# A two-pass channel gate: last load of pass one split in two, first scaling pieces cut finer, pass two reordered

## The chip, the core and the metric

The kernel runs on one core of one Trainium2 chip. The metric is the device time in microseconds. TensorE is called PE in the profile, VectorE DVE, ScalarE ACT, GpSimd POOL and SyncE SP. A "row" below is one image row of the work's tiling: 384 bf16 values on each of 128 partitions, 98,304 bytes in all.

## The reference

```
B, H, W, C = x.shape            # 1, 384, 384, 384, bf16
g = jnp.einsum("bhwc->bc", x) / (H * W)
s = _sigmoid(g * w1d[0])        # k = 1: no neighbours, no padding
return x * s[:, None, None, :]
```

Every channel is averaged over all pixels, the average is scaled by one weight and put through a sigmoid, and the whole input is multiplied by that gate. No element of the output can be written before the last element of the input has been read.

## The kernel before, in words

The 147,456 pixels make 1152 rows. SBUF holds `ROWS` = 275 rows in one tile, `arena`; the input does not fit, so there are two passes.

**Pass one** loads all 1152 rows. PE adds each with a matmul of ones into one PSUM bank (`sum_rows`, L291). 780 "stream" rows are dropped after that, and 372 are kept: 59 raw, the others in groups that DVE folds from four rows into three rows' room (`fold`, L331), with ACT testing that the folding is without loss. The last loads of pass one are written out by hand in L495: pairs of a row number in `arena` and a length. `U`, `V`, `W`, `A`, `T`, `Y` name places in `arena` (108, 212, 232, 220, 259, 267); `take_raw` loads and sums. After row 1152 ACT makes the gate `s_bf` (L503) and copies it to PSUM (`s_ps`, L507).

**Pass two** stores 1152 rows and loads the 780 stream rows again, all from the one queue of SP: `load` (L267), `store` (L525). `scale` (L512) multiplies in place. DVE scales nearly everything and unfolds the groups (`unfold`, L535); POOL scales 13 raw rows, A+26 to A+38, beside DVE at the start. While POOL works, DVE reads the gate from PSUM, later from SBUF.

The order of pass two is made by a loop that runs when the program is built (L771 to L849). It keeps a clock of its own, takes costs per row for DVE and DMA, and appends scales, unfolds, loads and stores to each engine's list. `landed` (L692) says in which pieces DVE scales the raw rows, `alongside` (L700) what POOL scales and when its store is due; a piece with `end` True gets a store of its own. A load may be appended when rows of `arena` have been stored. Each engine then runs its list strictly in order, waiting on semaphores: SP waits for DVE or POOL ahead of a store, and for a store's landing ahead of a load that overwrites its rows. DMA number n of SP, counted from 0, signals the semaphore `f_SP` followed by n modulo 24.

Of the kernel before, what the change touches and what calls it, by code (L numbers as in the profile page):

```python
# [145 lines left out]
def kernel(  # L146
# [13 lines left out]
    B, H, W, C = x.shape  # L160
# [14 lines left out]
    U = 3 * PIECE + PAIRS * 3 * PAIR  # L175
    G0 = U + PAIR
    V = G0 + PAIRS * 3 * PAIR
    A = V + PAIR
    N_A = 39
    T = A + N_A  # L180
    Y = T + 2 * PIECE
# [14 lines left out]
    W = A + 3 * PIECE  # L196
# [63 lines left out]
    def raw(a):  # L260

        return c_raw + (a - U if a < G0 else PAIR + a - V if a < A else 2 * PAIR + a - W)
# [202 lines left out]
    LATE = [(W + 4, 8), (U, 8), (W + 12, 8), (W + 20, 7)]  # L465
# [25 lines left out]
    def take_raw(a, n):  # L491
        load(raw(a), a, n)
        return sum_rows(a, n)

    for a, n in [(V, 8), *LATE, (W, 4), (T, 4), (T + 4, 4), (Y, 4), (Y + 4, 2), (Y + 6, 2)]:  # L495
        step = take_raw(a, n)
        if a == Y - 4:
            fl.hold("DVE", 2 * N_DVE[1], step)
# [13 lines left out]
    def scale(a, n, eng="DVE", s=s_bf, after=()):  # L512
        v = arena[:, a : a + n, :]
        vec = nc.vector if eng == "DVE" else nc.gpsimd
        step = fl.add(
            eng,
            lambda: vec.tensor_tensor(  # L517
                out=v, in0=v, in1=s[:, None, :].to_broadcast([P, n, C]), op=Op.mult
            ),
            reads=rows(a, n) + ["s_bf" if s is s_bf else "bank0"], writes=rows(a, n), after=after,  # L520
        )
        if eng == "DVE":
            scales.append(step)
# [165 lines left out]
        return f  # L689


    for a, n, end in ((Y, 2, True), (Y + 2, 2, True), (Y + 4, 4, True), (U, 4, True), (U + 4, 4, True), (T, 8, True), (V, 8, True)):  # L692
        landed.append((a, raw(a), n, end))
    landed.append((W, raw(W), 8, True))
    landed.append((W + 8, raw(W + 8), 6, True))
# [1 line left out]

    alongside = deque()
    t = 1.0
    for a, n in ((A + 26, 4), (A + 30, 4), (A + 34, 5)):  # L700
        scale(a, n, "POOL", after=[copied])
        t += 0.2 + 0.84 * n
        alongside.append((t, a, raw(a), n))
# [67 lines left out]
    while True:  # L771

        if dve_at <= now:
# [4 lines left out]
            if landed and (ahead < PENDING or not can):  # L778
                a, at, n, end = landed.popleft()
# [13 lines left out]
        if alongside and alongside[0][0] <= now:  # L793
            _, a, at, n = alongside.popleft()
# [3 lines left out]
        while waiting and waiting[0][0] <= now:  # L798
            _, n, then, at, a, known = waiting.popleft()
# [10 lines left out]
        if bank_at is None and len(line) <= total - BANKS_AT and got and max(got)[0] >= N_BANKED:  # L810
            a = max(got)[1]
# [11 lines left out]
        if got and todo < N_STREAM:  # L823
            n, a = max(got)
            left = N_STREAM - todo
            left -= run_of(left - 1)[0]
            n = min(n, CAP, left)
# [57 lines left out]
```

## Time and profile before

| | |
|---|---|
| median of three runs | 719.55 us (719.46 to 719.58) |
| the profiled execution: its own time / its span | 718.83 us / 717.1 us |
| busy: DVE / PE / ACT / POOL | 475.2 / 213.0 / 121.4 / 10.2 us |
| SP's DMA queue | 303.18 MB, 99.1% of 16 engines' span |
| mean rate | 423 GB/s |

The profile cuts the span into windows; for each it gives the busy time of every engine, the granted clock of PE, the mean busy share of the 16 DMA engines and the GB/s moved. The chain of waits follows back from the last instruction what each step waited for. The timeline lists instructions by start and length. SP's entries (SPq) are the issuing of DMAs, not the transfers.

### The profile page before, as it was taken

The page shows a single profiled execution, that of the slowest core. Times are in us where ns is not written, and L with a number is a line of the kernel's source. Part 1 is how long each engine was busy: PE and PEld are TensorE (multiplying, and loading weights), DVE is VectorE, ACT ScalarE, POOL GpSimd, SP SyncE. Part 2 cuts the span into 40 slices and gives each one's busy share as a digit, 9 for nine tenths or more (in the row PEclk, how much of TensorE's full clock was granted, in tenths as well). Part 3 has the DMA queues.
Part 4 walks back from the last instruction along what each step waited for, and adds up shares of the span by engine and source line. Part 5 has one row for each costly group of instructions (what it writes and reads, how often), then busy time and mean ns, then how long its engine had stood idle before and what let it go on. Part 6 is the DMA issues. An engine that isn't in the chain of part 4 may idle for free.

```text
span 717.1 us, 2040 instructions
## 1 busy us (share of the span) xinstructions
PE 213.0 (30%) x1186; PEld 0.3 (0%) x3; DVE 475.2 (66%) x355; ACT 121.4 (17%) x97; POOL 10.2 (1%) x7
## 2 busy tenths in 40 slices
PE   4776978998869780000000000000000000000000
PEld 0000000000000000000000000000000000000000
DVE  4606280639896829999999999779966960128900
ACT  3704160426674610000110000000000000000000
POOL 0000000000000005000000000000000000000000
PEclk9998989999999996555555555555555555555555
DMA  9999999999999989999999999999999999999997
GB/s 373 436 426 440 424 442 426 439 429 420 428 430 425 427 358 355 406 424 431 433 428 422 444 424 445 423 439 428 439 420 435 433 433 436 436 432 431 437 421 343
DMA packets 21038, 303.31 MB, mean 423 GB/s; under 512 B 2338, under 2 KB 2850, under 8 KB 9378
## 3 DMA queue, kind: packets, MB, share of 16 engines
q1 hardware_dynamic: 21024, 303.18, 99.1%
q8 instruction: 4, 0.07, 0.0%
q14 instruction: 8, 0.07, 0.0%
q10 hardware_dynamic: 2, 0.00, 0.0%
HBM read 189.92 MB, written 113.25 MB: 423 GB/s over the span
## 4 chain that ended last, share of the span: by engine, by line
DMA 56%; DVE 23%; PE 7%; another core or an unknown queue 3%; ACT 2%; POOL 1%; SPq 1%; issue 0%; DVEq 0%
DMA arena<-in_x_dram 45%; DVE arena L517 17%; DMA out_dram<-arena 11%; PE bank L280 7%; DVE arena L315 4%; ACT arena L352 2%; DVE arena L321 2%; POOL arena L517 1%; SPq L274 1%; SPq L531 0%; ACT s_bf L503 0%; ACT bank L507 0%; ACT bank L429 0%; DVEq L124 0%
## 5 line engine op out<-in xcount | busy, mean ns | idle before, releaser
L517 DVE TENSOR_TENSOR arena<-arena,s_bf 128x6144 bf16<-128x6144 bf16 (+13 forms) x67 | 226.9, 3424 | 86.1 <-DMA arena<-in_x_dram 71.0
L280 PE MATMUL bank<-arena,ones 128*128 128x384 bf16 x1151 | 207.2, 342 | 46.2 <-DMA arena<-in_x_dram 45.6
L315 DVE TENSOR_SCALAR arena<-arena 128x1536 uint16<-128x1536 uint16 (+4 forms) x193 | 136.9, 763 | 107.6 <-DMA arena<-in_x_dram 94.9
L352 ACT ACTIVATE arena<-arena 128x3072 uint16<-128x3072 uint16 (+1 forms) x38 | 107.6, 2831 | 111.6 <-DVE arena L315 111.6
L321 DVE TENSOR_TENSOR arena<-arena 128x1536 uint16<-128x1536 uint16 (+3 forms) x81 | 106.3, 1312 | 8.4 <-PE bank L280 5.2
L597 PE MATMUL bank<-odd,ones 128*128 128x1 bf16 x1 | 0.2, 184 | 262.2 <-DVE odd L592 262.2
L429 ACT COPY arena<-bank 128x512 uint32<-128x512 uint32 (+3 forms) x9 | 4.4, 497 | 86.6 <-DMA out_dram<-arena 86.3
L517 POOL TENSOR_TENSOR arena<-arena,s_bf 128x1536 bf16<-128x1536 bf16 (+1 forms) x3 | 9.9, 3345 | 269.2 <-ACT bank L507 269.2
L517 DVE TENSOR_TENSOR arena<-arena,bank 128x1536 bf16<-128x1536 bf16 (+3 forms) x8 | 9.4, 1248 | 0.0
L429 ACT COPY bank<-arena 128x512 uint32<-128x512 uint32 (+3 forms) x9 | 4.1, 489 | 26.5 <-PE bank L280 26.5
L352 ACT ACTIVATION_READ_ACCUMULATOR arena<-arena 128x1 f32 x38 | 7.1, 186 | 0.0
L280 PE MATMUL bank<-zeros,ones 128*128 128x384 bf16 x32 | 5.5, 326 | 0.0
L503 ACT ACTIVATE s_bf<-bank,w_sc 128x384 bf16<-128x384 f32 x1 | 0.6, 580 | 13.6 <-PE bank L280 13.6
L294 PE MATMUL bank<-arena,ones 128*128 128x384 bf16 x1 | 0.5, 477 | 7.1 <-DMA arena<-in_x_dram 7.1
L853 ACT ACT_TABLE_LOAD x1 | 1.3, 1283 | 0.7 <-PEq L869 0.7
L384 DVE TENSOR_SCALAR w_sc<-bank 128x1 f32<-128x1 f32 x1 | 0.2, 159 | 1.4 <-PE bank L379 1.4
L379 PE MATMUL bank<-w_bf,ones 1*128 1x1 bf16 x1 | 0.2, 183 | 2.4 <-DMA w_bf<-in_w1d_dram 2.4
L374 DVE MEMSET ones<- 128x128 bf16 x1 | 0.2, 165 | 1.0 <-SPq L118 1.0
L601 DVE CAST odd_i<-bank 128x1 int32<-128x1 f32 x1 | 0.2, 159 | 0.3 <-PE bank L597 0.3
L507 ACT COPY bank<-s_bf 128x192 uint32<-128x192 uint32 x1 | 0.3, 323 | 0.0
L597 PEld LDWEIGHTS bank<-odd,ones 128*128 128x128 bf16 x1 | 0.1, 102 | 521.0 <-DVE odd L592 521.0
L587 DVE TENSOR_REDUCE worst<-seen 128x1 f32<-128x38 f32 x1 | 0.2, 184 | 0.0
(8 smaller groups left out, 0.9 us busy)
## 6 DMA issues: line engine op xcount, KB each, us to landing
arena<-in_x_dram SPq DMA_DIRECT2D x18, 4608.0 KB, 31.8
out_dram<-arena SPq DMA_DIRECT2D x9, 4608.0 KB, 34.5
out_dram<-arena SPq DMA_DIRECT2D x7, 3072.0 KB, 23.6
arena<-in_x_dram SPq DMA_DIRECT2D x5, 3072.0 KB, 15.2
arena<-in_x_dram SPq DMA_DIRECT2D x13, 1152.0 KB, 17.1
arena<-in_x_dram SPq DMA_DIRECT2D x6, 2304.0 KB, 20.1
arena<-in_x_dram SPq DMA_DIRECT2D x15, 768.0 KB, 7.7
arena<-in_x_dram SPq DMA_DIRECT2D x2, 4128.0 KB, 38.2
```

The costliest lines, as they stand in the source:

```text
L274: lambda: nc.sync.dma_start(out=arena[:, a : a + hi - lo, :], in_=view(xf, *run)[:, lo:hi, :]),
L280: return pe.add_instruction(mybir.InstMatmult(name=nc.get_next_instruction_name(), ins=[pe.lower_ap(rhs), pe.lower_ap(ones[:])], outs=[pe. ...
L294: return nc.tensor.matmul(acc, lhsT=ones[:], rhs=arena[:, i, :], start=first, stop=last)
L315: lambda: nc.vector.tensor_scalar(out=dst, in0=src, scalar1=s0, scalar2=s1, op0=op0, op1=op1),
L321: "DVE", lambda: nc.vector.tensor_tensor(out=dst, in0=a, in1=b, op=op), reads=reads, writes=writes
L352: lambda: nc.scalar.activation(out=y, in_=y, func=ACTF.Copy, accum_out=seen[:, 2 * k + i : 2 * k + i + 1]),
L429: "ACT", lambda: nc.scalar.copy(dst.bitcast(u32), src.bitcast(u32)), reads=reads, writes=writes
L503: lambda: nc.scalar.activation(out=s_bf[:], in_=acc, func=ACTF.Sigmoid, scale=w_sc[:, 0:1]),
L507: "ACT", lambda: nc.scalar.copy(s_ps.bitcast(u32), s_bf[:].bitcast(u32)), reads=["s_bf"], writes=["bank0"]
L517: lambda: vec.tensor_tensor(out=v, in0=v, in1=s[:, None, :].to_broadcast([P, n, C]), op=Op.mult),
L597: lambda: nc.tensor.matmul(votes, lhsT=ones[:], rhs=odd[:], start=True, stop=True),
L853: nc.scalar.preload_act_table(ACTF.Sigmoid)
```

## The change

Three lists are edited, nothing else: the last two-row load of pass one becomes two loads of one row; the piece of four rows that DVE scales third becomes two pieces of two rows; POOL's pieces of 4, 4 and 5 rows become 2, 3, 4 and 4.

```diff
-    for a, n in [(V, 8), *LATE, (W, 4), (T, 4), (T + 4, 4), (Y, 4), (Y + 4, 2), (Y + 6, 2)]:
+    for a, n in [(V, 8), *LATE, (W, 4), (T, 4), (T + 4, 4), (Y, 4), (Y + 4, 2), (Y + 6, 1), (Y + 7, 1)]:
...
-    for a, n, end in ((Y, 2, True), (Y + 2, 2, True), (Y + 4, 4, True), (U, 4, True), (U + 4, 4, True), (T, 8, True), (V, 8, True)):
+    for a, n, end in ((Y, 2, True), (Y + 2, 2, True), (Y + 4, 2, True), (Y + 6, 2, True), (U, 4, True), (U + 4, 4, True), (T, 8, True), (V, 8, True)):
...
-    for a, n in ((A + 26, 4), (A + 30, 4), (A + 34, 5)):
+    for a, n in ((A + 26, 2), (A + 28, 3), (A + 31, 4), (A + 35, 4)):
```

The loop that orders pass two reads these lists, and rows come free in other pieces and at other moments of its clock, so the order of all of pass two is made anew.

SP's list where pass one ends and pass two begins. Loads go from `in_x_dram` to `arena`, stores from `arena` to `out_dram`; 128x384 is one row.

```order
-L274 DMA arena<-in_x_dram 128x768 x2
-L531 DMA out_dram<-arena 128x768 x2
-L531 DMA out_dram<-arena 128x1536 x4
+L274 DMA arena<-in_x_dram 128x768
+L274 DMA arena<-in_x_dram 128x384 x2
+L531 DMA out_dram<-arena 128x768 x5
+L531 DMA out_dram<-arena 128x1536 x2
+L531 DMA out_dram<-arena 128x1152
 L531 DMA out_dram<-arena 128x3072 x2
 L531 DMA out_dram<-arena 128x1536
 L531 DMA out_dram<-arena 128x3072
 L531 DMA out_dram<-arena 128x2304
```

Two of the four-row stores, one of them POOL's, become smaller ones; of the five stores of two rows the fifth is POOL's, and the store of three rows is POOL's too.

DVE's list at the same place (`bank_71` is the gate's copy in PSUM).

```order
 L517 TENSOR_TENSOR arena<-arena,s_bf 128x768
-L517 TENSOR_TENSOR arena<-arena,bank_71 128x768
-L517 TENSOR_TENSOR arena<-arena,bank_71 128x1536 x3
+L517 TENSOR_TENSOR arena<-arena,bank_71 128x768 x3
+L517 TENSOR_TENSOR arena<-arena,bank_71 128x1536 x2
 L517 TENSOR_TENSOR arena<-arena,bank_71 128x3072 x3
 L517 TENSOR_TENSOR arena<-arena,bank_71 128x2304
```

One scale of four rows became two of two; the rest of the first 46 rows is as it was.

SP's list from the 12-row store of the first unfolded group on, with the semaphores that it waits for, before.

```order
L531 DMA out_dram<-arena 128x4608 [waits f_DVE]
L531 DMA out_dram<-arena 128x3072 [waits f_DVE] x2
L274 DMA arena<-in_x_dram 128x1920 [waits f_SP21]
L274 DMA arena<-in_x_dram 128x1536 [waits f_SP1]
L274 DMA arena<-in_x_dram 128x3072 [waits f_SP2]
```

The same place in the list after the change.

```order
L531 DMA out_dram<-arena 128x4608 [waits f_DVE]
L531 DMA out_dram<-arena 128x1920 [waits f_DVE]
L531 DMA out_dram<-arena 128x3072 [waits f_DVE]
L274 DMA arena<-in_x_dram 128x1536 [waits f_SP5]
L531 DMA out_dram<-arena 128x3840 [waits f_DVE]
```

Both times the load of four rows waits for the landing of the 12-row store (`f_SP1`, `f_SP5`). Between the two stood 16 rows of stores and a load of 5 rows; now there are 13 rows of stores, and a store of 10 rows stands behind the load. In all, pass two has 37 loads as before, and 60 stores where there were 58.

## The prediction

> **What bounds the kernel now.** I read the page first, for the share of the DMA engines.
>
> ```profile
> DVE  4606280639896829999999999779966960128900
> DMA  9999999999999989999999999999999999999997
> GB/s 373 436 426 440 424 442 426 439 429 420 428 430 425 427 358 355 406 424 431 433 428 422 444 424 445 423 439 428 439 420 435 433 433 436 436 432 431 437 421 343
> q1 hardware_dynamic: 21024, 303.18, 99.1%
> ```
>
> The DMA engines are at nine tenths or more in 38 of 40 slices, and one queue fills 99.1% of the span. 303.18 MB is just 1932 rows loaded and 1152 stored, at 98,304 bytes, and neither number changes. So time can be won or lost only where the engines stand, where they move slowly, and by what each DMA costs on top of its bytes. The low slices are the first, the two around the passes' border (358, 355), one after it (406) and the last.
>
> The windows show the border and some places to compare with; the columns that count are the last two, DMA share and GB/s.
>
> ```profile
> 260.00:265.00 5.00, 4.39 (x27) 0.00 (x0) 0.00 (x0) 0.00 (x0) 0.00 (x0) 1.00 1.02 411
> 265.00:268.00 3.00, 2.68 (x16) 0.00 (x0) 0.00 (x0) 0.00 (x0) 0.00 (x0) 1.00 0.47 177
> 268.00:270.60 2.60, 0.55 (x4) 0.00 (x0) 1.40 (x3) 0.90 (x2) 0.99 (x1) 1.00 0.01 3
> 270.60:271.60 1.00, 0.00 (x0) 0.00 (x0) 1.00 (x2) 0.00 (x0) 1.00 (x1) 1.00 0.99 373
> 271.60:272.00 0.40, 0.00 (x0) 0.00 (x0) 0.40 (x2) 0.00 (x0) 0.40 (x1) 1.00 0.28 104
> 272.00:275.00 3.00, 0.00 (x0) 0.00 (x0) 3.00 (x3) 0.00 (x0) 3.00 (x2) 0.64 1.03 415
> 280.00:284.00 4.00, 0.00 (x0) 0.00 (x0) 3.93 (x5) 0.00 (x0) 0.00 (x0) 0.50 1.04 423
> 284.00:286.00 2.00, 0.00 (x0) 0.00 (x0) 1.97 (x2) 0.00 (x0) 0.00 (x0) 0.50 0.97 265
> 286.00:290.00 4.00, 0.00 (x0) 0.00 (x0) 3.91 (x5) 0.00 (x0) 0.00 (x0) 0.50 1.03 430
> 290.00:292.00 2.00, 0.00 (x0) 0.00 (x0) 2.00 (x2) 0.00 (x0) 0.00 (x0) 0.50 0.99 288
> 420.00:460.00 40.00, 0.00 (x0) 0.00 (x0) 39.69 (x17) 0.00 (x0) 0.00 (x0) 0.50 1.01 433
> 713.00:717.10 4.10, 0.00 (x0) 0.00 (x0) 0.00 (x0) 0.00 (x0) 0.00 (x0) 0.50 0.06 24
> ```
>
> The reader sees three things. The engines stand for 2.6 us up to 270.6, while the last rows are summed, the gate is made and the first scale runs. They work for 1.0 us, then stand again in most of 271.6 to 272.0, and never after that until 713. And in two stretches of 2 us, at 284 and 290, the engines are busy but move only 265 and 288 GB/s beside 423 and 430 in their neighbours.
>
> **The change part by part.** *The split load.* The chain of waits and the line of the last loads:
>
> ```profile
> 257.67 9.39 DMA arena<-in_x_dram
> 267.05 0.04 issue
> 267.09 1.47 PE bank L280 x8
> 268.59 0.59 ACT s_bf L503
> L274 SPq DMA_DIRECT2D arena<-in_x_dram x2: 432/432/433, 258.1 to 258.6; - x2
> DMA to landing us min/median/max: 9.4/9.4/9.4
> ```
>
> The last three loads (4, 2 and 2 rows) land at 267.05, 267.5 and 268.0. PE runs the last eight matmuls without a gap from 267.09. At 1.47 us for eight, of which about 0.3 is the last one's own end, they start 0.16 apart: the seventh at 268.07, the eighth at 268.23. So the last load is not what PE waits for; it is the four-row load before it, then PE's own pace. One-row loads let the seventh matmul be released a little earlier and nobody uses it. No row of before shows a one-row load. If two of them take no longer than one of two rows, the last lands at 268.0; if each takes as long as a two-row load (0.5 us later each), at 268.5, 0.3 past the eighth matmul's start. I take 0, because small size costs little: the four- to eight-row loads of 260 to 265 move at 411 GB/s, the long transfers of 420 to 460 at 433. Bounds 0 and +0.3 us. The extra issue on SP, 0.43 us at about 259, lies 9 us before its data; nothing is queued behind it that could run yet.
>
> *The finer first pieces.* The timeline and the groups at the border:
>
> ```profile
> 269.20 0.56 DVE L517 TENSOR_TENSOR arena<-arena,s_bf 128x768 bf16<-128x768 bf16 x1 [14.33 <-ACT s_bf L503]
> 269.68 3.14 DVE L517 TENSOR_TENSOR arena<-arena,bank 128x768 bf16<-128x768 bf16 x4
> 269.61 9.95 POOL L517 TENSOR_TENSOR arena<-arena,s_bf 128x1536 bf16<-128x1536 bf16 x3 [269.16 <-ACT bank L507]
> L517 DVE TENSOR_TENSOR arena<-arena,bank 128x768 bf16<-128x768 bf16 x1 | 0.5, 546 | 0.0
> L517 DVE TENSOR_TENSOR arena<-arena,bank 128x1536 bf16<-128x1536 bf16 x3 | 2.7, 948 | 0.0
> L517 POOL TENSOR_TENSOR arena<-arena,s_bf 128x1536 bf16<-128x1536 bf16 x2 | 6.2, 3104 | 269.2 <-ACT bank L507 269.2
> L517 POOL TENSOR_TENSOR arena<-arena,s_bf 128x1920 bf16<-128x1920 bf16 x1 | 3.8, 3825 | 0.0
> 269.79 0.35 SPq L531 DMA_DIRECT2D out_dram<-arena  x1
> 270.25 0.36 SPq L531 DMA_DIRECT2D out_dram<-arena  x1
> 271.12 0.33 SPq L531 DMA_DIRECT2D out_dram<-arena  x1
> DMA to landing us min/median/max: 1.8/1.8/1.8
> ```
>
> The last row is the first store's alone. It is issued at 269.79 and the engines start near 270.6, so 0.8 to 0.85 us lie between; two stores of two rows fill 270.6 to 271.6, 0.5 us each; so of the 1.8 us some 1.3 are not data. The third store, four rows, is issued only at 271.12 because DVE takes 0.95 us for its piece; its data begin 0.85 later, at 271.97. That is the second hole: 0.40 us with a share of 0.28, 0.29 us lost.
>
> After the change DVE's pieces (0.546 and 0.948 us, each beginning 0.08 before its forerunner's end, as 3.14 for the four shows against 3.39 added up) end at 270.23, 270.69, 271.15, then 272.02 and 272.88. POOL goes up by 0.72 us per row from 3.10 to 3.83, so two rows take 1.66 and three 2.38: ends at 271.27 and about 273.6. With 0.03 to issue and 0.85 to begin, the queue would get data at 271.57, 272.03, 272.4 (POOL's), 272.9, 273.75, 274.5 (POOL's); it runs out, without them, at 271.6, 272.1, 272.6, 273.1, 274.05 and 275.0. Each arrives in time, the first by only 0.03 us, so the hole goes: -0.29 us (bounds 0 and -0.29). What is late next is nothing until the 8-row pieces, as before. POOL's whole work grows by one start, about 0.2 us, and DVE's by 0.06; behind them wait the first unfolds, and those have several microseconds of queued transfers as cover.
>
> *Each DMA more.* In 260 to 265 mostly four-row loads move at 411 GB/s, in 420 to 460 far longer transfers at 433. Four rows (393,216 bytes) take 0.957 and 0.908 us at these rates: 0.05 us per DMA. Pass two has two stores more: +0.10 (bounds 0 and +0.2).
>
> The Trainium skill ("DMA: Bandwidth & Descriptors", Bandwidth, the measured part) says to batch DMAs to 1 MiB or more for 75% of peak, from a fit of 2.0 us for each plus its bytes at 436 GB/s; both figures are for DMAs issued from GpSimd. By it two more small stores would be an estimated +4.0 us. The 415 GB/s of 272 to 275, with stores of 0.2 to 0.4 MB one after another, disagrees.
>
> *The new order.* A load that waits for a store's landing holds SP's list, and stores already scaled wait behind it. That pauses the engines when less is queued behind the awaited store than the 1.3 us that landing and a new start take. The tightest place is the 12-row store and the four-row load after it. Before, 21 rows stood between; now 13. At 433 GB/s a row is 0.227 us, so 13 rows are 2.95 us and 1.65 are left. I take 0; bounds 0 and +3 (the load released late by all that stands there).
>
> ```profile
> SPq L274 <- DMA out_dram<-arena: 100.7, 20, 10.6
> L531 SPq DMA_DIRECT2D out_dram<-arena x1: 333/333/333, 680.2 to 680.2; - x1
> DMA to landing us min/median/max: 35.5/35.5/35.5
> ```
>
> SP waits long for stores today too (100.7 us in all) and the engines do not stand: such waits cost nothing in themselves. At the end the last store, 43 rows, is issued at 680.2 and lands 35.5 us later, of which 9.8 are its data. Some 24 us of cover hide the last scale. The new list also ends with a 43-row store, behind 48-row ones, so the drain after 713 stays.
>
> *The slow stretches.* 2 us at 265 and 2 us at 288 where 430 is usual cost 0.77 and 0.66, 1.43 us. Their cause does not show. The order there becomes another one. I take no change; bounds -1.43 and +1.43.
>
> Sum: 0 - 0.29 + 0.10 + 0 + 0 = -0.19 us. The profiled execution takes 718.83 us, the span of 717.1 and 1.7 around it; it would take 718.6. The median of the runs lies 0.72 above the profiled one, so 719.36, that is **719.4 us**.
>
> **The rivals.** *The slow stretches go* (719.36 - 1.43 = 717.9; one alone, 718.6). For it: they are tied to nothing that the change keeps, and the 5-row store and the loads issued there are cut anew. Against it: small transfers remain. Chance 0.13. *Two more of them come*: 720.8, chance 0.07.
>
> *SP's issuing becomes the bound, slower.*
>
> ```profile
> 279.58 1.25 SPq L531 DMA_DIRECT2D out_dram<-arena  x1
> 280.88 1.23 SPq L274 DMA_DIRECT2D arena<-in_x_dram  x1
> ```
>
> Here issues that follow one another take 1.25 and 1.23 us instead of 0.35. If the fourth to eighth store did (2, 2, 4, 4 and 3 rows, 0.5, 0.5, 0.95, 0.95 and 0.7 us of data), the engines would stand 0.75 + 0.75 + 0.3 + 0.3 + 0.55 = 2.65 us: 722.0. It decides from 0.5 us per issue on. Against it: 0.35 and 0.36 for the first two. Chance 0.07.
>
> *POOL's short pieces are not short*: if two and three rows take 3.1 us like four, SP stands at the fifth store until 272.75, its data come at 273.6 instead of 272.6, and the three-row store brings 0.6 more: +1.6, 721.0. It decides when two rows take over 2.1 us. Against it: the step from four to five rows. Chance 0.05.
>
> *The tight load opens a hole*: up to +3, 722.4, if 13 rows are not enough. Chance 0.05. *Each small DMA stands alone*, paying 1.3 us as the first store does: the two added ones +2.6, 722.0; chance 0.03, as the 1.03 share of 272 to 275 denies it. This is the skill's fixed cost per DMA ("DMA: Bandwidth & Descriptors", Bandwidth), which the trace there does not bear out.
>
> **How the numbers follow.** The forecast keeps 0.60. What a measurement of this kernel tells from no change is about 0.2%, 1.4 us: below 718.1 or above 721.0. Faster by that needs both slow stretches gone: 0.10 of the 0.13. Slower: issuing 0.07, the tight load 0.04, fixed cost 0.03, half of POOL's and a part of the added slow stretches 0.03, in all 0.17. Within: 0.73. The range 718.0 to 721.0 leaves out about 0.04 below and 0.15 above.
>
> **What would show it.** Right: in the windows no hole near 271.7 and a share of 1.0 from the first store on; the last matmul still at 268.5; POOL's first piece near 1.7 us; no window under 0.9 share before 713. Wrong: a dip of the share at 272.5 (POOL or SP), near 295 (the tight load), or other windows of 265 to 290 GB/s with a full share.

## The result and the profile after

The changed kernel takes 720.57 us (median of 22 runs, 719.45 to 722.37), the kernel before beside it 719.55 (22 runs, 718.60 to 720.05). The ratio is 1.0015, 95% interval 1.0009 to 1.0021: slower by about 1.1 us, where 0.2 us faster was forecast. The profiled execution takes 721.15 us with a span of 719.3, that of before 718.83 and 717.1. As much as 0.45 us of that distance stands already at the end of pass one (last four-row load landed at 267.50 instead of 267.05) and differs from run to run.

The page of the changed kernel, the same rows as before:

```profile
DMA  9999999999999989999999999999999999999997
GB/s 370 447 417 446 431 433 420 445 427 423 425 429 426 425 341 368 399 408 430 424 430 432 425 411 439 428 437 435 434 435 432 433 431 431 436 422 446 429 437 333
q1 hardware_dynamic: 21456, 303.18, 99.2%
```

The engines are as full as before and move the same bytes. Lower are the slices from 287 to 324 us (399 and 408; before 406 and 424) and the one from 414 to 432 (411; before 424): a full share and fewer GB/s. The windows of the changed kernel:

```profile
270.60:271.60 1.00, 0.00 (x0) 0.00 (x0) 1.00 (x4) 0.00 (x0) 1.00 (x1) 1.00 0.51 192
271.60:272.00 0.40, 0.00 (x0) 0.00 (x0) 0.40 (x2) 0.00 (x0) 0.40 (x2) 1.00 1.06 396
272.00:275.00 3.00, 0.00 (x0) 0.00 (x0) 3.00 (x4) 0.00 (x0) 3.00 (x2) 0.81 1.05 406
284.00:286.00 2.00, 0.00 (x0) 0.00 (x0) 1.97 (x2) 0.00 (x0) 0.00 (x0) 0.50 0.99 266
290.00:292.00 2.00, 0.00 (x0) 0.00 (x0) 2.00 (x3) 0.00 (x0) 0.00 (x0) 0.50 1.07 368
299.00:301.00 2.00, 0.00 (x0) 0.00 (x0) 1.97 (x2) 0.00 (x0) 0.00 (x0) 0.50 1.03 360
307.00:311.00 4.00, 0.00 (x0) 0.00 (x0) 3.80 (x4) 0.00 (x0) 0.00 (x0) 0.50 1.01 344
414.00:430.00 16.00, 0.00 (x0) 0.00 (x0) 15.50 (x9) 0.00 (x0) 0.00 (x0) 0.50 1.01 408
713.00:719.30 6.30, 0.00 (x0) 0.00 (x0) 0.00 (x0) 0.00 (x0) 0.00 (x0) 0.50 0.35 152
```

And those windows of before that were not shown yet:

```profile
299.00:301.00 2.00, 0.00 (x0) 0.00 (x0) 2.00 (x2) 0.00 (x0) 0.00 (x0) 0.50 1.02 412
307.00:311.00 4.00, 0.00 (x0) 0.00 (x0) 3.93 (x6) 0.00 (x0) 0.00 (x0) 0.50 1.04 430
414.00:430.00 16.00, 0.00 (x0) 0.00 (x0) 15.83 (x6) 0.00 (x0) 0.00 (x0) 0.50 1.00 430
```

The first store's data now begin near 271.1, and from there the share stays at 1.0: the second hole is gone. The stretch at 284 has stayed. Three windows are new: 299 to 301, 307 to 311 and 414 to 430, with the engines full and the rate down. Against the rates of before they cost 2 x (1 - 360/412) = 0.25, 4 x (1 - 344/430) = 0.80 and 16 x (1 - 408/430) = 0.82, together 1.9 us. The first holds the lone four-row load that the prediction called the tight load, the second a 10-row load, the third a 39-row load. The stretch at 290 is still there too, only later: 292 to 294 now has 329 GB/s, before 436.

The chain of waits and the groups of GpSimd at the border:

```profile
258.11 9.40 DMA arena<-in_x_dram
267.50 0.04 issue
267.55 1.47 PE bank L280 x8
L517 POOL TENSOR_TENSOR arena<-arena,s_bf 128x1536 bf16<-128x1536 bf16 x2 | 6.1, 3085 | 0.0
L517 POOL TENSOR_TENSOR arena<-arena,s_bf 128x1152 bf16<-128x1152 bf16 x1 | 2.4, 2364 | 0.0
L517 POOL TENSOR_TENSOR arena<-arena,s_bf 128x768 bf16<-128x768 bf16 x1 | 1.7, 1655 | 269.6 <-ACT bank L507 269.6
```

PE again waits for the four-row load, then runs eight matmuls in 1.47 us without a gap. GpSimd's pieces of two and three rows take 1.66 and 2.36 us.

### The profile page after: what moved, and what is told of

It is laid out like the page before. It is cut to its first block, busy times and chain, and to the rows that moved or that the text cites. A ratio compares the mean times of both kernels' runs of the same rounds, so it can differ in the third digit from the quotient of the medians.

```text
span 719.3 us, 2048 instructions
## 1 busy us (share of the span) xinstructions
PE 213.8 (30%) x1186; PEld 0.3 (0%) x3; DVE 475.3 (66%) x356; ACT 121.4 (17%) x97; POOL 10.3 (1%) x8
## 4 chain that ended last, share of the span: by engine, by line
DMA 63%; DVE 20%; PE 7%; ACT 2%; SPq 1%; issue 0%; DVEq 0%
DMA arena<-in_x_dram 43%; DMA out_dram<-arena 20%; DVE arena L517 14%; PE bank L280 7%; DVE arena L315 4%; ACT arena L352 2%; DVE arena L321 1%; SPq L274 1%; ACT s_bf L503 0%; ACT bank L429 0%; PE bank L597 0%; DVE odd L592 0%; DVE odd_i L601 0%; DVE worst L587 0%; DVEq L124 0%
## 5 line engine op out<-in xcount | busy, mean ns | idle before, releaser
L517 DVE TENSOR_TENSOR arena<-arena,s_bf 128x6144 bf16<-128x6144 bf16 (+11 forms) x67 | 226.8, 3423 | 83.9 <-DMA arena<-in_x_dram 68.9
L517 POOL TENSOR_TENSOR arena<-arena,s_bf 128x1536 bf16<-128x1536 bf16 (+2 forms) x4 | 10.1, 2547 | 269.6 <-ACT bank L507 269.6
L517 DVE TENSOR_TENSOR arena<-arena,bank 128x768 bf16<-128x768 bf16 (+3 forms) x9 | 9.5, 1125 | 0.0
```

The lines of the kernel that those rows point to most:

```text
L517: lambda: vec.tensor_tensor(out=v, in0=v, in1=s[:, None, :].to_broadcast([P, n, C]), op=Op.mult),
```

## The experiments

All ratios are to the kernel before on the same chip. They stand in three groups: which part of the change costs, what could undo it, and whether the time of a load's issue makes it slow.

**The order or the pieces.** One kernel takes the new pieces and puts the order of before behind them, one the old pieces and the new order behind them. Both write the pieces and their stores out by hand and let the planning loop pass them over.

```diff
+    first = ((Y + 4, 2), (Y + 6, 2)) if FINE else ((Y + 4, 4),)
+    byhand = [(Y, 2), (Y + 2, 2), *first, (U, 4), (U + 4, 4), (T, 8), (V, 8), (W, 8), (W + 8, 6)]
...
-            store(at, a, n)
...
+            if at < c_raw:
+                known.append(store(at, a, n))
```

> The new pieces at the border (loads of 1 and 1 row, VectorE 2, 2, 2, 2, GpSimd 2, 3, 4, 4, and the stores in the changed order up to the first load of pass two), but all of pass two behind them in the order of the kernel before. Theory O (the new order of pass two brings more slow stretches): no loss, 0.1 to 0.4 us faster than before, as the predicted sum had it. Theory P (the small pieces themselves cost, later, by what they leave in the queue): +0.8 to +1.2 us, like the changed kernel. Theory R (slow stretches fall by chance, whatever the order): as before within 0.4 us, and the changed kernel too would come near it on this chip.

> The pieces of before at the border (one load of 2 rows, VectorE 2, 2, 4, GpSimd 4, 4, 5), and behind them pass two in the order of the changed kernel. Theory O: slower than before by 1.0 to 1.6 us, since the order is kept and the 0.3 us of the second hole come back. Theory P: as before within 0.3 us. Theory R: as before within 0.4 us.

New pieces, old order: 719.47 us, ratio 1.0000 (0.9991 to 1.0009). Old pieces, new order: 720.70 us, 1.0018 (1.0010 to 1.0027). The windows of the first, then of the second:

```profile
299.00:301.00 2.00, 0.00 (x0) 0.00 (x0) 2.00 (x2) 0.00 (x0) 0.00 (x0) 0.50 1.06 425
307.00:311.00 4.00, 0.00 (x0) 0.00 (x0) 3.93 (x5) 0.00 (x0) 0.00 (x0) 0.50 1.04 430
```

```profile
299.00:301.00 2.00, 0.00 (x0) 0.00 (x0) 1.97 (x2) 0.00 (x0) 0.00 (x0) 0.50 1.00 350
307.00:311.00 4.00, 0.00 (x0) 0.00 (x0) 3.65 (x3) 0.00 (x0) 0.00 (x0) 0.50 1.01 384
```

The loss and two of the slow windows go with the new order, not with the small pieces.

**The two kernels again**, unchanged, beside these:

> The changed kernel once more, for a second profile. Theory O: slow windows (under 300 GB/s with a full DMA share) again at the ends of runs of loads between 284 and 312 us, in the same places of the list as in the first profile (the last 4-row store, the 8-row load before the 12-row store, the 10-row load before the 4-row store), and one or two more later on; 719.5 to 722 us. Theory R: slow windows at other places of the list.

> The kernel before once more, for a second profile. Theory O: slow windows again at the last store before the first load and at the 10-row load, about 1.4 us in all, and hardly any elsewhere; 718.6 to 720.1 us. Theory R: at other places, and as many as in the changed kernel.

720.44 us, 1.0013 (1.0004 to 1.0021), and 719.53 us, 1.0000 (0.9991 to 1.0009). The loss repeats, with 359 GB/s at 299 to 301, 374 at 307 to 311 and 419 at 414 to 430; the kernel before has 416, 428 and 426 there. The slow windows stand in the same places of the list as in the first profiles, though less deep than the 300 GB/s expected.

**One part of the change alone**: the split load, DVE's pieces, GpSimd's pieces, each of the three edited lines by itself in the kernel before.

> Only the last load of pass one as two of one row; everything else as before, pass two in the old order. Both theories (order, and order by GpSimd's pieces alone): as before, ratio 1.000 within 0.0006, the first scale at the same distance from the third-last landing. A theory that the one-row loads hold up the sum would give +0.3 us at most.

> Only VectorE's third piece cut in two. The list of pass two comes out in a third order (30 switches between loads and stores where before has 26 and the changed kernel 28, counting runs of one kind). If the number of switches were what counts: slower than the changed kernel, +1.5 us over before. If it is where single loads stand: anything from 0 to +1.2, to be read from the slow windows.

> Only GpSimd's pieces as 2, 3, 4, 4. The list behind the border is word for word that of the changed kernel. Theory order: +1.0 to +1.4 us over before, slow windows at 284, 291, 299 and 308 us as in the changed kernel. If VectorE's pieces were needed for the loss: as before.

Split load 719.46 us, 0.9997 (0.9989 to 1.0006); DVE's pieces 719.36, 0.9998 (0.9990 to 1.0007); GpSimd's pieces 721.25, 1.0025 (1.0016 to 1.0034). DVE's pieces lead to a third order with 30 changes between loads and stores, against 26 before and 28 after, and lose nothing: the number of changes alone is not the cause. GpSimd's pieces alone bring, behind the border, SP's list of the changed kernel word for word, and its loss (1.7 us, more than the 1.0 to 1.4 expected). Of its windows 307 to 311 (368) and 414 to 430 (420) are slow again, but 299 to 301, which was expected slow, has 406.

**Undoing it.** Three tries: the new pieces with fewer and larger loads (a load is held until 12 rows are free; its row is cut here), and in the changed kernel the lone four-row load moved behind two stores and the next load, and the 10-row load ahead of a five-row one.

```diff
-    BIG, CAP, LOW, LAST = 32, 48, 9.0, 4.0
+    BIG, CAP, LOW, LAST = 32, 48, 9.0, 3.5
...
+                if nth == SWAPPED:
+                    held = (lo, a, n)
+                else:
+                    load(lo, a, n)
+                    if held:
+                        load(*held)
```

> The new pieces at the border, and behind them an order in which loads are held until 12 rows are free and the planner's queue is under 3.5 us (before: 8 rows, 4.0 us): 144 DMAs in all instead of 149, and one switch less in the first 100 us. Theory order: five DMAs fewer than the changed kernel are -0.25 us, the second hole is gone as there; with slow windows as in before 719.0 us, 0.4 under before; with more of them up to 720. If small pieces cost by themselves: 720.5.

> The changed kernel with one step of SP's list moved: the load of four rows that stands alone between stores (waits for the 12-row store) now stands behind the next two stores and the 8-row load. Theory place (a load is slow where a store follows it): the slow window at 299 to 301 us is gone, the same rows load at full speed inside the run of loads; 0.3 us less, 720.2. Theory rows (its addresses make it slow): a slow window at about 305 us instead, no gain.

> The changed kernel with two neighbours in SP's list swapped: the load of ten rows, slow in both profiles at 307 to 311 us, stands ahead of the load of five rows, which is now the one that a store follows. Theory place: the ten-row load is fast and the five-row one slow, the dip shorter and a little later, 0 to 0.4 us less. Theory rows: the ten-row load is slow as before, the dip begins 1 to 2 us earlier, no gain.

Fewer loads: 720.08 us, 1.0014 (1.0003 to 1.0024), a miss. Load behind: 721.77, 1.0038 (1.0024 to 1.0052, 6 runs), a miss in the time. Loads swapped: 720.86, 1.0024 (1.0015 to 1.0033), a miss. The windows of the kernel with the load behind:

```profile
299.00:301.00 2.00, 0.00 (x0) 0.00 (x0) 1.97 (x2) 0.00 (x0) 0.00 (x0) 0.50 1.04 439
307.00:311.00 4.00, 0.00 (x0) 0.00 (x0) 3.93 (x7) 0.00 (x0) 0.00 (x0) 0.50 1.05 436
318.00:326.00 8.00, 0.00 (x0) 0.00 (x0) 7.90 (x8) 0.00 (x0) 0.00 (x0) 0.50 1.02 376
```

The same four rows, loaded to the same place in `arena`, are fast now, and so is the 10-row load, which stands where it stood: neither its rows nor its length makes a load slow. But another stretch, at 318 to 326, has come instead (376; 433 after the change), and the whole is slower still. In the kernel with fewer loads the same window has 388. In that with the loads swapped 307 to 311 falls to 294: the 10-row load is slow though a load follows it, as the theory of rows had it. But it is issued 1.94 us before its first packets there, and 5.00 us before them in the kernel where it is fast.

**The time of issue.** Of a load, call lead the time from its issue to its first packets. A short lead is the suspect that these kernels leave, and five others try it. The first makes a 24-row load of before, until then issued 12 us ahead, wait for the landing of 20 rows of a store; the second has the same pieces without the wait (`FIRST_PART` is 20).

```diff
+            if (a, n) == (60, 32):
+                known.append(store(at, a, FIRST_PART))
+                late.append(known[-1])
+                known.append(store(at + FIRST_PART, a + FIRST_PART, n - FIRST_PART))
...
-            writes=rows(a, hi - lo), dma=True,
+            writes=rows(a, hi - lo), dma=True, after=late[:1],
```

> The kernel before with one place changed: the 32-row store that SP issues at about 349.4 us is issued as 20 and 12 rows, and the 24-row load behind it, until now issued at once and about 12 us before the engines reach it, also waits for the landing of the 20 rows. It is then issued about 2 us before the engines run out of stores. Theory lead (a load that is issued 1.2 to 2.2 us before the engines come to it runs at about half speed, wherever it stands and whatever its rows): this load, which is fast in every profile so far, becomes slow for some microseconds, a window under 400 GB/s with a full share of the engines between about 360 and 370 us; 0.4 to 1.0 us more than the control. Theory place (the rows or the place in the list make a load slow): no such window, and the time of the control within 0.4 us. If the engines stand there instead (a share under 0.9), the wait was too tight to decide anything.

> The kernel before with the same 32-row store issued as 20 and 12 rows, and no added wait: the 24-row load behind it is issued at once as before. Both theories: 435 GB/s between 360 and 370 us, and the time of before plus about 0.05 us for one DMA more, so 719.3 to 719.8 us.

720.88 us, 1.0026 (1.0017 to 1.0035), against 719.56, 0.9998 (0.9988 to 1.0007). The added wait costs 1.3 us. But the load that waited ran nearly at full speed; slow was the end of the load two places behind it, the last one before the stores. Its window with the wait, then in the control:

```profile
374.00:377.00 3.00, 0.00 (x0) 0.00 (x0) 3.00 (x2) 0.00 (x0) 0.00 (x0) 0.50 1.08 356
```

```profile
374.00:377.00 3.00, 0.00 (x0) 0.00 (x0) 3.00 (x2) 0.00 (x0) 0.00 (x0) 0.50 1.02 430
```

So the expectation held in the time and failed in the place: the load that became slow had a lead of 7.62 us itself, 6.88 in the control. The next three go to the dearest load, 39 rows, the last before a 32-row store. In the changed kernel it is issued early, by putting the 25-row store that it waits for ahead of the 36-row load; in the kernel before it is issued late, by making it wait for the first 36 rows of the 48-row load ahead of it; the control has that cut without the wait (`FIRST_PART` is 36 there).

```diff
+                if (a, n) == (68, 36) and not swapped:
+                    held.append((lo, a, n))
...
+            while held:
+                load(*held.pop())
```

```diff
+                if (a, n) == (68, 48) and not cut:
+                    first = load(lo, a, FIRST_PART)
+                    load(lo + FIRST_PART, a + FIRST_PART, n - FIRST_PART)
+                    late.append(first)
```

> The changed kernel with two neighbours in SP's list swapped: the 25-row store, on whose landing the 39-row load waits, stands ahead of the 36-row load instead of behind it. The 39-row load should be issued at about 404 us instead of 412.6, some 10 us before the engines reach it instead of 2. Theory lead: its slow stretch at 421 to 424 (about 1.0 us in the profile of the changed kernel, 0.72 in that of its second run) goes, no window from 414 to 430 under 415 GB/s with a full share, and the time is 0.5 to 1.0 us under the changed kernel's 720.5, so 719.5 to 720.0. Theory place (its rows or its place between 24 rows of stores and a 32-row store make it slow): the stretch stays, 720.3 to 720.8. Two more changes of direction come with the swap, both with over 25 rows queued; if each change costs something by itself, it is slower than 720.8.

> The kernel before with the 48-row load that it issues at about 399 us cut into 36 and 12 rows, and the 39-row load behind it, the last before a 32-row store, made to wait for the landing of the 36 rows. It is then issued at about 418 us instead of 404.8, about 2 us before the engines reach it instead of 15. Theory lead: it becomes slow for some microseconds between 419 and 433, 0.4 to 1.0 us more than the control. Theory place: no slow window there and the control's time within 0.4 us. In between: if only the coming from stores to loads and back with a short queue matters, it stays fast, since it comes behind 72 rows of loads.

> The kernel before with the same 48-row load as 36 and 12 rows and no added wait. Both theories: as before, 719.3 to 719.9 us, no slow window between 400 and 440.

For each the issue of this load (start, duration) in the timeline and the window in which it runs. The changed kernel:

```profile
412.61 0.34 SPq L274 DMA_DIRECT2D arena<-in_x_dram  x1
```

The changed kernel with the load early:

```profile
403.88 0.34 SPq L274 DMA_DIRECT2D arena<-in_x_dram  x1
414.00:430.00 16.00, 0.00 (x0) 0.00 (x0) 15.93 (x10) 0.00 (x0) 0.00 (x0) 0.50 1.02 438
```

The kernel before with the load late:

```profile
418.42 0.33 SPq L276 DMA_DIRECT2D arena<-in_x_dram  x1
414.00:430.00 16.00, 0.00 (x0) 0.00 (x0) 16.00 (x6) 0.00 (x0) 0.00 (x0) 0.50 1.00 394
426.00:430.00 4.00, 0.00 (x0) 0.00 (x0) 4.00 (x2) 0.00 (x0) 0.00 (x0) 0.50 0.94 277
```

Its control:

```profile
404.68 0.33 SPq L276 DMA_DIRECT2D arena<-in_x_dram  x1
414.00:430.00 16.00, 0.00 (x0) 0.00 (x0) 16.00 (x6) 0.00 (x0) 0.00 (x0) 0.50 1.00 429
426.00:430.00 4.00, 0.00 (x0) 0.00 (x0) 4.00 (x2) 0.00 (x0) 0.00 (x0) 0.50 0.97 418
```

Issued early, the load is fast in the changed kernel (438 GB/s instead of 408 and 419 in its two profiles); issued late, it is slow in the kernel before (394 instead of 429, with 277 for four microseconds), while its rows, its length and the list around it are those of the control. One thing comes with the wait: it holds SP's list, so the 32-row store behind the load is issued late too, at 418.79 us instead of 407.21. In the changed kernel with the load early that store moves by only 2.3 us (410.67 instead of 412.99), and the load by 8.7. Late costs 721.26 against 719.31 us, 1.0028 (1.0017 to 1.0038) against 0.9998 (0.9989 to 1.0007): 1.95 us. Early gives 720.22 us, 1.0008 (0.9999 to 1.0017): the stretch is gone, but the time fell by only 0.2 to 0.35 us from the changed kernel's 720.44 to 720.57, less than the 0.5 expected at least, and the intervals overlap, so that a gain in time is not shown. The window at 299 to 301 is still there in it, at 359.

This one load, over all profiles in which it has a lead under 3 us, by the packet records (lost: the time of its 128 packets above 27.07 GB/s and 8.3 ns for each, divided by 16 engines; the two figures are about what fast packets of before take):

| kernel | lead, us | lost, us |
|---|---|---|
| before, issued late | 1.57 | 1.29 |
| after, second run | 2.02 | 0.72 |
| after | 2.08 | 1.00 |
| GpSimd's pieces alone | 2.16 | 0.63 |
| new order, old pieces | 2.51 | -0.02 |
| load behind | 2.70 | 0.27 |
| loads swapped | 2.75 | 0.01 |

With a lead of 9.7 us and more (after with the load early, before, the controls and the rest) it lost at most 0.07.

Another load shows that the lead is not all. The 10-row load near 308 us has leads of 2.78 to 3.16 us in four profiles of the new order and lost 0.36 to 0.73 us; with leads of 2.81 to 3.14 in the eight profiles of the old order that have a 10-row load there, it lost nothing. In the old order it stands alone between stores, in the new one it comes behind two other loads.

Summed over all transfers from 275 to 660 us, 2.25 us are lost in the profile of the changed kernel and 0.30 in that of before. The difference of 1.95 us is about that from the first store's data to the last packet, 446.55 us against 444.68: in these two executions the slow transfers account for what pass two lost. Elsewhere the two figures agree less closely (1.14 and 0.30 us above before with the 39-row load early).

## Why the prediction was wrong

*The split load*, 0: right. PE's eight matmuls follow the four-row load as before; alone it gives 0.9997.

*The finer first pieces*, -0.29: right in mechanism. The hole is closed, and 1.66 and 2.38 us had been worked out for GpSimd's pieces that took 1.66 and 2.36. The gain is too small to be seen in a median: new pieces with the old order give 1.0000.

*Each DMA more*, +0.10: no run contradicts it, and none could show so little. (By the traces pass two has 30 loads in both kernels, not 37; the two added stores are right.) The two controls have one DMA more than before and lie at 719.56 and 719.31 us beside 719.58 and 719.46, with at most 0.5 us more by their intervals. The 2.0 us for each DMA issued from GpSimd that the Trainium skill ("DMA: Bandwidth & Descriptors", Anatomy of one DMA — SWDGE (gpsimd) path) states are not paid here, where SP issues. The page gives this fit apart from its rule of 1 MiB, which the prediction took to follow from it.

*The new order*, 0, and *the slow stretches*, 0: here it failed. What the prediction asked of a load that waits for a store was only whether the engines run empty before its data come. They did not: at 299 to 301 the share is 1.03. But the tight load, which comes in time (issued at 297.57, at its turn near 299.4), runs slowly, and so do the 10-row load, issued 2.8 us before its turn, and the 39-row load, issued 2.1 us before. The step that failed is the term for slow stretches, left at no change while the list around them was made anew. I had the row that warns of it, 2 us at 288 GB/s on a load of before, wrote that its cause does not show, and left the term at zero, with a chance of 0.07 for two more such stretches (720.8 us). That rival is what came: in the profile three more, worth 1.9 us, in the median about 1.1.

*The rivals.* SP's issuing did not become the bound at the border, GpSimd's short pieces were short, no hole opened at the tight load, and small DMAs did not stand alone. Of the signs that were to show it wrong the last came: other windows of low rate with a full share, as low as 285 GB/s in one of 2 us (422 to 424, share 0.91) and 317 in another (309 to 311, share 0.97).

*The size of a measurement.* The 0.2% taken as no change was fair: 1.0 to 1.1 us is 0.15%, which needed 22 runs of each. The median lay inside the range; the side was wrong.

What stays open: why the engines are slow there. Shown is that the loss goes with the new order, that making the 39-row load wait (and with it SP's list behind it) makes it slow, that issuing it early makes it fast, and that making an earlier load wait can bring the same to a load two places behind. The lead of the slow load by itself does not explain all: not explained are the 10-row load near 308, the stretch at 284, a last store before a load with a lead of 4 us, which is slow in every kernel tried, and that at 290, with a lead of 5 us. At 318 to 326 a 24-row load with a lead of 2.21 us lost 0.87 us in the kernel with fewer loads, which fits a short lead. In that with the load behind a 10-row store with a lead of 0.90 lost 0.85, but a 24-row load with one of 5.00 lost 0.76 as well. No kernel tried beats the one before by more than the intervals: the lowest ratios are 0.9997 (split load) and 0.9998 (DVE's pieces, two controls).

## What to carry to other kernels

When one queue keeps the DMA engines full, ask of each transfer not only whether it comes before the engines run empty, but how long before its turn it was issued: here, over the 17 profiles, 9 of 10 last loads before a change to stores were slow (0.25 us or more lost) with a lead under 2.3 us. A longer lead was no guarantee, since 25 of 118 were slow with 2.3 to 10 us, 16 of them the one near 290 us. A list that is ordered anew changes these leads far from the edit, so compare issue times and rates by window over the whole span, not only at the edited place. A stretch with a full share and a low rate is a cost whose cause is to be found before the order is touched, not a constant.

## What the runs showed of the hardware

Over the 17 profiles, the transfers of pass two that ran between 275 and 660 us were sorted afterwards, a transfer being called slow if it lost 0.25 us or more. Of 864 that were followed by one of the same direction, one was slow, the 10-row load of the kernel with the loads swapped (lead 1.94 us, lost 0.81). Of those that were the last before the direction changes, 51 of 186 were slow where fewer than 25 rows (5.7 us) were queued when they were issued, 3 of 271 where more were. Of the last loads with a lead under 2.3 us, 9 of 10 were slow, 0.58 us in the mean; with a lead over 10 us 2 of 99, neither above 0.30. In the window at 299 the slow load's packets took 1.35 times as long as usual in the mean: most took their usual time, about one in six over 1.3 times as long, up to 5.6 times. Those of the store running beside them took their usual time. This sorting was made to fit the data; only the cases of the 24-row and the 39-row load were set up to test it.

The two one-row loads land at 268.21 and 268.48, 0.25 and 0.27 us behind what is ahead of them, half of the 0.5 us of a two-row load (267.50 to 267.96): the split costs the engines nothing.
